# Retention followed by a two-layer leaky-ReLU network: who casts units 6 and 7, when units 10 and 11 are loaded, and where three tile bursts stand

## The chip, the cores and the metric

The kernel runs on one core of a Trainium2 chip. The metric is the device time of one execution in microseconds (us); lower is better. Five engines of the core run their own instruction lists side by side and meet at semaphores: TensorE (PE in the profile; PEld is its weight load), VectorE (DVE), ScalarE (ACT), GpSimd (POOL) and SyncE (SP, used here for transfers alone). Transfers are issued from the SP and POOL queues.

## The reference

```python
# q, k, v: 8 batches, 8 heads, 576 positions, 64 wide; float32
scores = scale * np.matmul(q, k.transpose(0, 1, 3, 2))
gamma = 1.0 - 2.0 ** (-5.0 - np.arange(H, dtype=np.float32))
Dmat = np.where(rel >= 0, gamma[:, None, None] ** rel[None, :, :], 0.0)
ret = scores * Dmat[None, :, :, :]
attn = np.matmul(ret, v)                      # retention, causal with decay
x = attn.transpose(0, 2, 1, 3).reshape(4608, 512)
h = x @ w_in                                  # 512 -> 2048
g = np.maximum(0.01 * h, h)
out = g @ w_out                               # 2048 -> 512, float32
```

## The kernel before

**Units.** The 4,608 tokens are cut into 36 units of 128 tokens (two chunks of 64). Retention is done chunk by chunk with a running state. For each unit u the steps are: `loads(u, eng)` brings k, q and v (three transfers of 256 KB, in this order) into float32 tiles `t`, of which five sets exist; `casts(u)` turns them into float16 (`cast_k` on ScalarE, L157; q and v multiplied by a decay table `cs` through `scaled`, L160, on VectorE where u < NEARLY and on GpSimd otherwise). The transposed q and k (`qkT`) come for u below NPE = 7 from TensorE (`transposes(u)`, L197, copied out at L203), and for later units from a transposing DMA that `cast_q` issues on SP (L171). `scores(u)` (L216, L225) fills one PSUM tile `sc`, of which there is one; `masks(u)` (L234) and `states(u)` (L252 to L257) read it on VectorE, so the next `scores` waits for them; `state_copy(u)` (L268) makes a float16 state, on ScalarE below NACT = 8 and on GpSimd from there on; `outputs(u)` (L323, L334) does 32 small matmuls into `ot`, ScalarE copies one half into `own` (L342), VectorE adds both into `xT` (L346).

**Groups.** The two layers run over groups of 256 tokens (two units). `g1_blocks(g)` gives eight blocks of 8 matmuls from `xT` and `w_in` into `hps` (L455, two buffers), each followed by ScalarE's leaky ReLU into `gt` (L462). `g2_blocks(g)` gives eight blocks of 4 matmuls from `gt` and `w_out` into `yps` (L478), a VectorE copy into `osb` (L488) and a store on SP (L490). The first group that goes wholly through the regular loop is group 3 (units 6 and 7), "layer one's fourth group"; its `g1_blocks(3)` needs `xT` of units 6 and 7.

**Order.** Every engine does its instructions in the order in which they are written; nothing reorders them. Up to L656 the order is written out by hand. From L657 `run(upto, *lists)` mixes the blocks of two lists by position and places "bursts" of unit work between them: burst n, from `steady(n)`, is `scores(n)`, `outputs(n-1)` (from n = 9 on), `masks(n)`, `states(n)`, then `casts(n+3)` (from n = 9 on), then `loads(n+6)` on SP. The call at L657 has ten blocks, eight of `g1_blocks(3)` and the last two of `g2_blocks(2)`, and bursts 8, 9 and 10; its blocks come in the order g1, g1, g2, g1, g1, g1, g1, g2, g1, g1. The line that places the bursts is

```python
run_steps(min(upto, a + -(-(upto - a) * (m + 1) // max(1, len(order) - 3)), done + 1))
```

With ten blocks and three bursts it puts burst 8 behind block 1, burst 9 behind block 3 and burst 10 behind block 5. In the next call burst 11 stands behind its first block, a `g1_blocks(4)` block that needs `xT` of units 8 and 9.

**GpSimd's queue.** Units 1 to 11 are loaded by GpSimd, with the weights between. Before a transfer `ring` keeps at most ten pieces of 256 KB in flight: it takes the oldest off by copying one element of it on GpSimd into `probe` (L132), which waits for that piece to land. Besides, the program as built has eight semaphores in turn for GpSimd's transfers, so each waits for the eighth before it. Behind L623 stand in GpSimd's list: loads of unit 9; casts of 6 and 7; loads of 10; casts of 8; loads of 11; casts of 9, 10 and 11. A load of unit u overwrites the float32 tiles of unit u-5, and so waits for that unit's casts.

Of the kernel before, what the change touches and what calls it, by code (L numbers as in the profile page):

```python
# [17 lines left out]
def kernel(  # L18
# [23 lines left out]
    nc = tc.nc  # L42
# [65 lines left out]

    NPE = 7
    NFIRST = 8  # L110
    NEARLY = 6
    NACT = 8
    NRING = 11
    t32 = {}
# [7 lines left out]
    def half(i):  # L122
        return slice(CH * i, CH * i + CH)
# [14 lines left out]
    def load(u, x, eng):  # L138
        t = ld_pool.tile([P, H, D], FP, name=f"t32_{x}")
        t32[u, x] = t  # L140
        (b0, c0), (b1, c1) = units[u]
        src = (q, k, v)[x]
        parts = [(t, b0, c0, P)] if b0 == b1 else [(t[0:CH], b0, c0, CH), (t[CH:P], b1, c1, CH)]
        for dst, b, c, n in parts:
            if eng is nc.gpsimd:
                ring(H * n * D * 4, dst[0:1, 0, 0:1])
            eng.dma_start(  # L147
                out=dst, in_=src[b, :, CH * c : CH * c + n, :].rearrange("h t d -> t h d")
            )

    def loads(u, eng):
        for x in (1, 0, 2):
            load(u, x, eng)

    def cast_k(u):
        qk16[u] = b_pool.tile([P, 2, H, D], F16, name="qk16")
        nc.scalar.copy(out=qk16[u][:, 1], in_=t32[u, 1])  # L157

    def scaled(u, x, out):
        (nc.vector if u < NEARLY else nc.gpsimd).tensor_tensor(  # L160
            out=out,
            in0=t32[u, x],
            in1=tab_sb[:, kind(u), x // 2, :].unsqueeze(2).to_broadcast([P, H, D]),
            op=MUL,
        )

    def cast_q(u):
        scaled(u, 0, qk16[u][:, 0])
        if u >= NPE:
            qkT[u] = b_pool.tile([P, 2, NP, P], F16, name="qkT")  # L170
            nc.sync.dma_start_transpose(  # L171
                out=qkT[u].rearrange("p x c t -> p (x c) t"),
                in_=qk16[u].rearrange("t x h d -> t (x h d)"),
            )

    def cast_v(u):
        v16[u] = b_pool.tile([P, H, D], F16, name="v16")
        scaled(u, 2, v16[u])

    def casts(u):  # L180
        if u >= NU:
            return
        cast_k(u)
        cast_q(u)
        cast_v(u)
# [86 lines left out]
    def st_before(u, j):  # L272

        if units[u][j][1] == 0:
            return zst
        if j:
            return st16[u][:, 0]
        return st16[u - 1][:, 1]
# [34 lines left out]
    def outputs(u):  # L313


        ot = ot_pool.tile([P, 2, 2 * NP, CH], FP, name="ot")
        own = ot[:, :, 0:NP]
        far = ot[:, :, NP : 2 * NP].rearrange("q r (s j) t -> q r s (j t)", j=2)
        for hp in range(NP):
            for h in (hp, hp + NP):  # L320
                o, c = divmod(h, NP)
                for j in range(2):
                    nc.tensor.matmul(  # L323
                        out=own[half(o), j, c, :],
                        lhsT=v16[u][half(j), h, :],
                        rhs=s16s[u][half(j), h % 2, h // 2, :],
                        start=True, stop=True, skip_group_check=True,
                    )
        for j in range(2):
            for s in range(2):  # L330
                for o in range(2):
                    for g in range(2):
                        p = 2 * o + s
                        nc.tensor.matmul(  # L334
                            out=far[half(o), g, s, half(j)],
                            lhsT=st_before(u, j)[half(g), p, :],
                            rhs=qkT[u][half(g), 0, p, half(j)],
                            start=True, stop=True, skip_group_check=True,
                        )
        t0 = P * u % XR  # L340
        tmp = a_pool.tile([P, NP, P], FP, name="own")
        nc.scalar.copy(  # L342
            out=tmp.rearrange("q c (j t) -> q c j t", t=CH),
            in_=own.rearrange("q j c t -> q c j t"),
        )
        nc.vector.tensor_tensor(  # L346
            out=xT[:, :, t0 : t0 + P].rearrange("q (s g) t -> q g s t", g=2),
            in0=far,
            in1=tmp.rearrange("q (s g) t -> q g s t", g=2),
            op=ADD,  # L350
        )
# [76 lines left out]
    ends = []  # L428
# [3 lines left out]
    done = 0  # L432

    def run_steps(upto):
        nonlocal done
        while done < upto:
            steps[done][1]()
            done += 1
# [4 lines left out]
    def g1_blocks(g):  # L443

        tok, t0 = sizes[g], starts[g]
        nf = TOK // tok

        def block(fb):
            if fb == 0:
                g_tiles[g] = g_pool.tile([P, NF, tok], F16, name=f"gt{tok}")  # L450
            hps = h_pool.tile([P, nf, tok], FP, name="hps")
            for f in range(nf):
                fc = fb * nf + f
                for c in range(NP):
                    nc.tensor.matmul(  # L455
                        out=hps[:, f, :],
                        lhsT=w_in16[:, c, fc * P : (fc + 1) * P],
                        rhs=xT[:, c, t0 % XR : t0 % XR + tok],
                        start=(c == 0),
                        stop=(c == NP - 1),  # L460
                    )
            nc.scalar.activation(  # L462
                out=g_tiles[g][:, fb * nf : (fb + 1) * nf, :], in_=hps,
                func=mybir.ActivationFunctionType.Lrelu,
            )

        return [lambda fb=fb: block(fb) for fb in range(NF // nf)]

    def g2_blocks(g, width=1):

        t0 = starts[g]

        def block(tbs, part):
            for f in range(4 * part, 4 * part + 4):
                for tb in tbs:
                    if f == 0:
                        y_cur[g, tb] = y_pool.tile([P, DM], FP, name="yps")
                    nc.tensor.matmul(  # L478
                        out=y_cur[g, tb],
                        lhsT=g_tiles[g][:, f, tb * P : (tb + 1) * P],  # L480
                        rhs=w_out16[:, f, :],
                        start=(f == 0),
                        stop=(f == NF - 1),
                    )
            if part == 3:
                for tb in tbs:
                    osb = o_pool.tile([P, DM], FP, name="osb")
                    nc.vector.tensor_copy(out=osb, in_=y_cur[g, tb])  # L488
                    r0 = t0 + tb * P
                    nc.sync.dma_start(out=out[r0 : r0 + P, :], in_=osb)  # L490

        return [
            lambda tb=tb, part=part: block(range(tb, tb + width), part)
            for tb in range(0, sizes[g] // P, width)
            for part in range(4)
        ]

    def run(upto, *lists):

        order = sorted(  # L500
            ((n + 0.5) / len(ls), x, n) for x, ls in enumerate(lists) for n in range(len(ls))
        )
        a = done
        for m, (_, x, n) in enumerate(order):
            lists[x][n]()
            run_steps(min(upto, a + -(-(upto - a) * (m + 1) // max(1, len(order) - 3)), done + 1))
        run_steps(upto)

    def g2_wide(tbs):
# [88 lines left out]
    def some(a, b):  # L598
        for m in range(a, b):
            wide[m]()  # L600

    g2 = g2_blocks(2)

    def more(blocks, a, b):
        for m in range(a, b):
            blocks[m]()
# [13 lines left out]
    scores(5)  # L620
    masks(5)
    states(5)
    loads(9, nc.gpsimd)  # L623
    casts(6)
    casts(7)
    some(9, 12)
    loads(10, nc.gpsimd)
    some(12, 13)
    outputs(5)
    some(13, 16)  # L630
    more(g1[2], 0, 1)
    transposes(6, sc_pool)
    casts(8)
    loads(11, nc.gpsimd)
    more(g1[2], 1, 3)
    scores(6)
    masks(6)
# [16 lines left out]
    more(g2, 1, 4)  # L654
    outputs(7)
    more(g2, 4, 6)  # L656
    run(ends[4], g1_blocks(3), g2[6:])  # L657
    for g in range(4, NG):
        run(ends[g + 1], g1_blocks(g), g2_blocks(g - 1))
    g2 = g2_blocks(NG - 1)  # L660
    run(ends[NG], g2[:4])
    for a, b in ((0, 3 * P), (3 * P, DM)):
        y = y_pool.tile([P, DM], FP, name="yps")
# [41 lines left out]
```

## Time and profile before

| what | value |
|---|---|
| median of 6 runs | 308.98 us (306.04, 306.64, 308.54, 309.42, 310.9, 311.46) |
| profiled execution, its own time | 306.04 us |
| its span, first to last instruction | 304.1 us |
| granted TensorE clock | 1.00 |
| busy PE / DVE / ACT / POOL | 291.6 / 107.0 / 138.1 / 121.5 us |
| bytes moved, mean rate | 50.26 MB, 165 GB/s |

How to read it: a busy time is the sum over an engine's instructions, a wait is idle time of an engine put down to the event that ended it. The chain of waits follows the work that ended last backwards from the last instruction. A mean over the span says little here, since the first quarter (loading, unit by unit) and the rest have different limits; so stages are read by windows of time.

### The profile page before, as it was taken

How to read it: one execution, taken by the hardware profiler on the slowest of the kernel's cores; microseconds unless marked ns; L12 is line 12 of the kernel's file. 1: busy time of each engine (PE TensorE's matmuls, PEld its weight loads, DVE VectorE, ACT ScalarE, POOL GpSimd, SP SyncE). 2: the span in 40 equal slices, each digit the busy share in tenths (PEclk: the TensorE clock that was granted, in tenths of full speed). 3: DMA queues.
4: the chain of work that ended last, by engine and by line, in shares of the span. 5: the costliest groups of instructions: out<-in, count | busy, mean ns of one | idle time of the engine just before them, and what ended most of it. 6: DMA issues, size and time to landing. Idle time of an engine off the chain costs nothing.

```text
span 304.1 us, 9489 instructions
## 1 busy us (share of the span) xinstructions
PE 291.6 (96%) x4169; PEld 197.1 (65%) x4169; DVE 107.0 (35%) x200; ACT 138.1 (45%) x240; POOL 121.5 (40%) x178
## 2 busy tenths in 40 slices
PE   3999999978999999999999999999999999999996
PEld 2478745736766666666666666666666666666663
DVE  1761153344442425152525143423333234331001
ACT  3577625834644444454535353535353534343320
POOL 8868869982533333333333333333333330000000
DMA  8999998899999995968496947685887221000011
GB/s 221 287 195 192 199 257 263 218 243 206 222 223 237 211 254 115 199 174 202 128 177 158 239 128 175 165 180 162 164 176 180 73 69 39 34 37 34 37 68 70
DMA packets 121400, 50.26 MB, mean 165 GB/s; under 512 B 110288, under 2 KB 114768, under 8 KB 121360
## 3 DMA queue, kind: packets, MB, share of 16 engines
q1 hardware_dynamic: 113952, 36.65, 52.1%
q0 software_dynamic: 6976, 12.85, 17.7%
q8 instruction: 32, 0.52, 0.7%
q10 hardware_dynamic: 432, 0.17, 0.3%
q14 instruction: 8, 0.07, 0.1%
HBM read 36.81 MB, written 9.44 MB: 152 GB/s over the span
## 4 chain that ended last, share of the span: by engine, by line
PE 76%; DMA 10%; POOL 9%; issue 2%; DVE 1%; ACT 1%; POOLq 0%; ACTq 0%
PE yps L478 34%; PE hps L455 34%; POOL t L147 6%; DMA w_out<-in_moe_w_out_dram 4%; DMA t<-in_k_dram 2%; PE sc L216 2%; DMA w_in<-in_moe_w_in_dram 2%; DMA t<-in_v_dram 2%; PE ot L334 1%; PE ot L323 1%; PE sc L225 1%; PE yps L665 1%; POOL qk L160 1%; POOL v L160 1%; POOL probe L132 1%
## 5 line engine op out<-in xcount | busy, mean ns | idle before, releaser
L455 PE MATMUL hps<-xT,w_in 128*128 128x256 f16 x1152 | 146.2, 273 | 2.5 <-DVE xT L346 1.9
L462 ACT ACTIVATE gt<-hps 128x512 f16<-128x512 f32 x144 | 85.7, 597 | 125.4 <-PE hps L455 125.1
L455 PEld LDWEIGHTS <-w_in 128*128 128x128 f16 x1152 | 112.1, 98 | 40.6 <-issue 3.0
L478 PE MATMUL yps<-w_out,gt 128*128 128x512 f16 x496 | 126.3, 380 | 0.0
L268 POOL CAST st<-s 128x512 f16<-128x512 f32 (+1 forms) x28 | 15.6, 557 | 137.4 <-DVE s L255 54.8
L478 PEld LDWEIGHTS <-gt 128*128 128x128 f16 x496 | 46.3, 98 | 34.3
L346 DVE TENSOR_TENSOR xT<-ot,own 128x512 f16<-128x512 f32 x32 | 22.1, 691 | 81.3 <-ACT own L342 81.3
L488 DVE COPY osb<-yps 128x512 f32<-128x512 f32 x31 | 21.3, 686 | 75.4 <-PE yps L478 75.4
L160 POOL TENSOR_TENSOR qk<-t,cs 128x512 f16<-128x512 f32 x30 | 31.3, 1043 | 1.2 <-DMA t<-in_q_dram 1.1
L160 POOL TENSOR_TENSOR v<-t,cs 128x512 f16<-128x512 f32 x30 | 31.3, 1042 | 0.0
L234 DVE TENSOR_TENSOR s<-sc,cs 128x512 f16<-128x512 f32 x36 | 24.6, 682 | 6.5 <-PE sc L225 5.0
L157 ACT CAST qk<-t 128x512 f16<-128x512 f32 x36 | 22.3, 621 | 4.2 <-DMA t<-in_k_dram 3.9
L342 ACT COPY own<-ot 128x512 f32<-128x512 f32 x32 | 18.7, 585 | 8.0 <-PE ot L334 6.1
L255 DVE TENSOR_TENSOR s<-sc,s 128x256 f32<-128x256 f32 x40 | 16.8, 419 | 0.7
L216 PEld LDWEIGHTS <-qkT 64*64 64x64 f16 x576 | 7.7, 108 | 11.3 <-issue 8.2
L216 PE MATMUL sc<-qkT 64*64 64x64 f16 x576 | 11.6, 199 | 1.8 <-DVE s L255 1.2
L147 POOL DMA_DIRECT2D t<-in_k_dram x12 | 10.5, 879 | 1.7 <-POOLq L689 0.8
L225 PE MATMUL sc<-v,qk 64*64 64x64 f16 x576 | 10.9, 194 | 0.0
L147 POOL DMA_DIRECT2D t<-in_v_dram x12 | 10.2, 850 | 0.3 <-issue 0.3
L147 POOL DMA_DIRECT2D t<-in_q_dram x12 | 10.2, 852 | 0.0
L523 PEld LDWEIGHTS <-gt 128*128 128x128 f16 x64 | 5.9, 98 | 6.3
L323 PE MATMUL ot<-s,v 64*64 64x64 f16 x512 | 9.8, 194 | 0.0
(52 smaller groups left out, 144.9 us busy)
## 6 DMA issues: line engine op xcount, KB each, us to landing
out_dram<-osb SPq DMA_DIRECT2D x35, 256.0 KB, 3.9
t<-in_k_dram SPq DMA_DIRECT2D x22, 256.0 KB, 3.3
t<-in_q_dram SPq DMA_DIRECT2D x22, 256.0 KB, 4.1
t<-in_v_dram SPq DMA_DIRECT2D x22, 256.0 KB, 4.1
t<-in_k_dram POOLq DMA_DIRECT2D x10, 256.0 KB, 5.2
t<-in_q_dram POOLq DMA_DIRECT2D x10, 256.0 KB, 5.5
t<-in_v_dram POOLq DMA_DIRECT2D x10, 256.0 KB, 5.4
w_in<-in_moe_w_in_dram POOLq DMA_DIRECT2D x8, 256.0 KB, 6.1
```

Of the source, the lines that this page charges most:

```text
L147: eng.dma_start(out=dst, in_=src[b, :, CH * c : CH * c + n, :].rearrange("h t d -> t h d"))
L157: nc.scalar.copy(out=qk16[u][:, 1], in_=t32[u, 1])
L160: (nc.vector if u < NEARLY else nc.gpsimd).tensor_tensor(out=out, in0=t32[u, x], in1=tab_sb[:, kind(u), x // 2, :].unsqueeze(2).to_broadca ...
L216: nc.tensor.matmul(out=a[half(j), g, 0, p, :], lhsT=qkT[u][half(g), 1, p, half(j)], rhs=qkT[u][half(g), 0, p, half(j)], start=True, stop=T ...
L234: nc.vector.tensor_tensor(out=s16s[u], in0=sc_tiles[u][:, :, 0], in1=mask_sb.unsqueeze(1).unsqueeze(1).to_broadcast([P, 2, NP, CH]), op=MUL,)
L255: nc.vector.tensor_tensor(out=dst, in0=st[:, j], in1=prev, op=ADD)
L342: nc.scalar.copy(out=tmp.rearrange("q c (j t) -> q c j t", t=CH), in_=own.rearrange("q j c t -> q c j t"),)
L346: nc.vector.tensor_tensor(out=xT[:, :, t0 : t0 + P].rearrange("q (s g) t -> q g s t", g=2), in0=far, in1=tmp.rearrange("q (s g) t -> q g s ...
L455: nc.tensor.matmul(out=hps[:, f, :], lhsT=w_in16[:, c, fc * P : (fc + 1) * P], rhs=xT[:, c, t0 % XR : t0 % XR + tok], start=(c == 0), stop ...
L462: nc.scalar.activation(out=g_tiles[g][:, fb * nf : (fb + 1) * nf, :], in_=hps, func=mybir.ActivationFunctionType.Lrelu,)
L478: nc.tensor.matmul(out=y_cur[g, tb], lhsT=g_tiles[g][:, f, tb * P : (tb + 1) * P], rhs=w_out16[:, f, :], start=(f == 0), stop=(f == NF - 1),)
L488: nc.vector.tensor_copy(out=osb, in_=y_cur[g, tb])
```

## The change

VectorE casts q and v of units 6 and 7, which GpSimd did; units 10 and 11 are issued by GpSimd straight behind unit 9, with no cast between them; the casts of unit 7 (ScalarE's k cast too) move behind `outputs(5)` in program order; and the one call at L657 places its bursts with `late=0`, which puts 8, 9 and 10 behind blocks 1, 4 and 7. No instruction's size changes, and the four casts keep their form.

```diff
-    NEARLY = 6
+    NEARLY = 8
...
-    def run(upto, *lists):
+    def run(upto, *lists, late=3):
...
-            run_steps(min(upto, a + -(-(upto - a) * (m + 1) // max(1, len(order) - 3)), done + 1))
+            run_steps(min(upto, a + -(-(upto - a) * (m + 1) // max(1, len(order) - late)), done + 1))
...
     states(5)
-    loads(9, nc.gpsimd)
+    for u in (9, 10):
+        loads(u, nc.gpsimd)
     casts(6)
-    casts(7)
     some(9, 12)
-    loads(10, nc.gpsimd)
+    loads(11, nc.gpsimd)
     some(12, 13)
     outputs(5)
+    casts(7)
     some(13, 16)
     more(g1[2], 0, 1)
     transposes(6, sc_pool)
     casts(8)
-    loads(11, nc.gpsimd)
...
-    run(ends[4], g1_blocks(3), g2[6:])
+    run(ends[4], g1_blocks(3), g2[6:], late=0)
```

GpSimd's list behind L623 then reads: loads of 9, 10 and 11; casts of 8, 9, 10 and 11. On SP the transposing DMA of unit 7 stood ahead of all four `osb` stores of groups 0 and 1; it now stands behind the first of them. `some(a, b)` are blocks of the second layer of groups 0 and 1 (L523, copied out at L532).

## Prediction

> **What bounds the kernel now.** I read the page's rate of work per stage first, by windows of time (columns: window, its length; busy us and count of PE, PEld, DVE, ACT, POOL; granted clock, DMA share, GB/s):
>
> ```profile
> 52.00:78.00 26.00, 22.42 (x433) 16.16 (x431) 10.53 (x20) 14.43 (x27) 19.18 (x27) 1.00 0.92 212
> 78.00:180.00 102.00, 102.00 (x1509) 69.46 (x1510) 37.32 (x71) 46.82 (x82) 35.92 (x42) 1.00 0.85 191
> ```
>
> From 78 us on TensorE never stands still: 102.00 of 102.00 us, at full clock. No edit here takes work from it, so whatever is won must be idle time before 78. TensorE's waits between 30 and 80 us (us in total, times, longest) are three:
>
> ```profile
> PE hps L455 <- DVE xT L346: 1.9, 1, 1.9
> PE sc L216 <- DVE s L255: 1.2, 1, 1.2
> PE hps L455 <- ACT gt L462: 0.5, 1, 0.5
> ```
>
> They sum to 3.57 us (1.87 + 1.16 + 0.54 in the timeline), the most this trace offers: 1.2% of 306.04. The chain of waits (start us, us, what) says what the largest is:
>
> ```profile
> 59.19 7.15 DMA t<-in_k_dram
> 66.34 0.02 issue
> 66.36 0.02 ACTq L157
> 66.38 0.04 issue
> 66.42 0.62 ACT qk L157
> 67.03 0.49 ACT own L342
> 67.53 0.02 issue
> 67.55 0.70 DVE xT L346
> 68.25 0.04 issue
> 68.29 1.03 PE hps L455 x8
> ```
>
> Unit 11's k is issued at 59.19 and lands at 66.34. ScalarE, in order, sits on its cast for 3.01 us; behind it is queued unit 7's `own` copy, ready since `outputs(7)` ended at 64.6; behind that VectorE's `xT` and the first block of layer one's fourth group. TensorE waits for a k tile that it needs some 15 us later. Why the load is that late is in GpSimd's timeline (start us, us, what):
>
> ```profile
> 50.02 1.05 POOL L160 TENSOR_TENSOR qk<-t,cs 128x512 f16<-128x512 f32 x1
> 51.03 1.04 POOL L160 TENSOR_TENSOR v<-t,cs 128x512 f16<-128x512 f32 x1
> 52.03 1.03 POOL L160 TENSOR_TENSOR qk<-t,cs 128x512 f16<-128x512 f32 x1
> 53.03 1.03 POOL L160 TENSOR_TENSOR v<-t,cs 128x512 f16<-128x512 f32 x1
> ```
>
> Four casts (units 6, 7) stand ahead of unit 10's loads, and two more (unit 8, 57.08 to 59.07) ahead of unit 11's.
>
> **Earlier loads.** Unit 9's last load ends at 49.93. A probe and an issue take 0.12 + 0.88, about 1.0 us (48.93 to 49.93). Six go through from there: unit 10's from 50.0, unit 11's k at about 53.1, the end at 56.0. Unit 11's k is thus issued 6.1 us earlier (six casts at 1.0 each); with the 7.15 us it took, it lands at 60.3. ScalarE reaches its cast after `state_copy(7)` at 63.4 and ends at 64.0, before `outputs(7)` does. Then `own` 64.6 to 65.2, `xT` to 65.9; TensorE finishes its second-layer blocks at 66.42 and waits no more: 1.87 us gone, with 0.5 us to spare, and landing has 4 us of slack. What is late next is the `own`–`xT` chain itself. The transfers fall where the DMA engines have room: between 52 and 56 us their share is 0.44 at 108 GB/s, against 1.02 at 334 GB/s from 44 to 48.
>
> The overwritten tiles: unit 11 needs unit 6's casts done. ScalarE's was done by 47.6; VectorE's two now run behind `states(5)`, from 46.4 to 47.7 if v of unit 6 (issued 40.81, median landing 5.2 us) is there. No wait.
>
> SP's queue: the transposing DMA of unit 7 goes at about 50.9, not 53.09; `scores(7)` wants it at 58.7. Units 8 to 11 follow GpSimd's casts, now 56.0 to 64, where unit 11's ended at 69.3; unit 8's has its q about 1 us earlier. Loads 12 and 13 on SP, behind unit 11's transposition, move from 69.65 to about 65, which hides them further. Unit 10's k had also been late by about 0.25 us at ScalarE (two casts in 1.37, where two at 47.01 take 1.13), so about 0.23 of the 0.54 us wait at 59.73 goes.
>
> **Four casts on VectorE.** By its own rows (L160 on VectorE, 0.68 to 0.69 us, pitch 0.60) they cost 2.5 us of VectorE, hidden in gaps: it idles from 46.39 to 48.45 and needs 1.3 for unit 6; unit 7's run behind `xT` of unit 5, 50.1 to 51.4, and push the second `osb` copy from 50.13 to 51.4, whose buffer is not wanted before 64. If the cover failed (v of unit 6 landing 8.4 us after issue or later, 49.25), `xT` of unit 5 would come after 51.3 and TensorE would wait one for one; the longest landing of these loads is 7.4 us, so I take 0, upper end 0.5. ScalarE's unit 7 cast behind `own` of unit 5 fits between 49.4 and 50.66: 0.
>
> VectorE casts beside GpSimd's list can lengthen both. The probes show it: 0.17 us as a rule, but one of 0.55 in the stretch 11.02 to 12.12 and one of 0.59 at 18.00, both while VectorE was at an L160 cast (17.88 to 18.56). The issues beside such casts keep 0.88 to 0.91 (29.34 to 31.99). So up to 0.42 us on each of four probes, 0 to 1.7 us on GpSimd; I take 0.8, which comes out of the 4 us of slack: 0 on TensorE.
>
> The Trainium skill, SBUF — State Buffer, section Who interferes with whom, has a rule against this edit: a VectorE instruction with two SBUF inputs and a GpSimd instruction that reads SBUF shut each other out, the second waiting for the first's end. The probe rows agree with it, and descriptor generation is spared there as in the rows of the issues; by its harsher sentence on a VectorE perf mode, which starves GpSimd's transfers, the four casts would hold GpSimd by 2.7 us, still inside the slack. The rule would speak loudest for casts beside casts, which no trace here shows.
>
> **The spread bursts.** Before, burst 10 follows burst 9 by 3.72 us, of which two blocks and the burst fill 2.56: `scores(10)` waits 1.16 for the one `sc` tile. The path burst start → `own` → `xT` → mask → states → next burst is 3.72 us (71.53 to 75.25) however the blocks stand. After, burst 8 to 9 has three blocks (3.1 us) where 2.27 are needed. From 9 to 10 there are three: 0.64 + 2.79 = 3.43, wait 0.29, so 0.87 is won. From 10 to 11, where there were six blocks, four: 0.84 + 3.58 = 4.42, needed 4.31 (75.25 to `states(10)` done at 79.42, and 0.14): no wait for `sc`, but GpSimd's `st` copy, 0.61, then holds `outputs(10)` as it holds `outputs(9)` now (0.84 for a burst against 0.64): 0.2 lost. The next group's first block needs `xT` of unit 9 2.3 us after burst 10 starts and comes after 3.4: covered.
>
> **Sum.** 1.87 + 0.23 + 0.87 − 0.2 = 2.77 us, about 2.8. The profiled execution would go from 306.04 to 303.2 (span 304.1 to 301.3). Both ends: 3.57 if every wait goes and no new one comes; 1.6 if the burst edit gives nothing and 0.5 is lost on `xT` of unit 5 (1.87 + 0.23 − 0.5).
>
> Against the median: that execution is the fastest of six, 2.94 below the median. Where the rest of them lose it no trace shows. The chain of waits is all GpSimd and DMA up to 68.29, TensorE is gapless at a clock of 1.00 from 78, so a slow transfer has one place to show: the wait for unit 11's k, for which the change makes 4 us of slack. If none of the 2.94 goes, the median becomes 306.2; if all, 303.2. I take half: 308.98 − 2.8 − 1.5 = 304.7.
>
> **Rivals.** *Another wait takes its place* (0.16). The removed wait was 1.87 us in which VectorE, GpSimd and SP caught up; with it gone the single `sc` tile sets bursts 9 to 11, or a transposed tile is late. For: burst 9 starts at 71.53, 0.15 after `states(8)` ended, so it is nearly tight already. Against: the spacing above. Then only some 0.9 of the 2.8 stay: 308.1.
>
> *GpSimd sticks in its loads* (slower, 0.12). Casts of units 8 to 11 are now behind six loads, each waiting for the eighth transfer before it. Unit 10's k needs unit 7's q, issued 42.56, by 50.0: 7.4 us, and the longest landing is 7.4. Crowded by these very loads, landings could stretch; at 11 us the last load ends near 59, unit 8's casts at 61, and its transposition (up to 7.9 us) at 68, 0.9 past `scores(8)` at 67.1. From there each us of landing costs about one: at 13 us the 2.8 are eaten, at 17 us the cost is 6.9 and the time 308.98 + 6.9 − 2.8 = 313.1. For: 334 GB/s and a share of 1.02 are already there from 44 to 48. Against: median 5.2 us there, and the empty stretch behind.
>
> *The bursts don't spread*: the built order has them behind blocks 1, 4, 7, so this falls away; if the spread is worth nothing, the gain is 2.1 and the time 305.4, inside the forecast.
>
> **How the numbers follow.** A run-to-run spread of this size cannot tell under about 1% from nothing: 305.9 to 312.1 is "the same". The forecast has 0.72; it spans 302.4 (3.57 with all of the surplus: 306.04 − 3.57) to 307.4 (308.98 − 1.6), and its middle, 304.7, is 1.2 below 305.9, so I give four fifths of it to faster: 0.58, and 0.14 to same. The first rival gives 0.16 same; the second is 0.12, taken as slower. The range, 302.0 to 309.0, holds the forecast and the first rival with some 0.4 to 0.9 of run-to-run spread beyond their ends, and leaves out the second.
>
> **What would show it.** Right: unit 11's k issued near 53 us; no wait of `hps` on `xT` near 66; the four casts on VectorE at 0.69 us; `scores(10)` waiting under 0.5 us; burst 11 near 78.5 instead of 81.42; the span near 301.3, gapless after. Wrong: GpSimd idle ahead of loads of 10 and 11 by more than 2 us; VectorE waiting on v of unit 6 past 49; a wait of `scores(8)` for its transposed tile; a span shorter by under 1 us; or the surplus of the slower runs staying whole, which puts the median near 306.2.

## The result, and the profile after

| | before | changed |
|---|---|---|
| median | 307.42 us (39 runs, 304.92 to 315.68) | 304.88 us (18 runs, 303.41 to 310.64) |
| ratio, with 95% interval | | 0.992 (0.9893 to 0.9946) |
| profiled execution, its own time | 306.04 us | 306.12 us |
| its span, mean granted clock | 304.1 us, 1.00 | 304.0 us, 0.994 |

The change makes the kernel 0.8% faster: 2.5 us of medians, and no more than the 1% named as the limit of telling. The ratios leave out executions over 1.5% above the fastest of their kernel, which the medians and ranges take in. The two profiled executions are equally long, so the second is not a typical one: TensorE's clock was halved in it for 3.4 us, which happens in some executions of both kernels.

The same stretches as before, by windows of time (window, its length; busy us and count of PE, PEld, DVE, ACT, POOL; granted clock, DMA share, GB/s), after:

```profile
52.00:78.00 26.00, 23.22 (x421) 15.79 (x419) 9.41 (x18) 13.49 (x25) 15.65 (x23) 0.93 1.07 244
78.00:180.00 102.00, 102.00 (x1520) 69.53 (x1521) 38.44 (x72) 47.27 (x82) 37.30 (x44) 1.00 0.86 188
```

From 78 us on nothing changed, 102.00 of 102.00. All that moved lies ahead of it, where the transfers' share rose from 0.92 to 1.07 and the clock fell to 0.93. Of TensorE's three waits one is left, and it has grown (us in total, times, longest us):

```profile
PE hps L455 <- ACT gt L462: 2.6, 1, 2.6
```

The chain of waits of the changed kernel (start us, us, what) says what is behind it:

```profile
52.11 7.45 DMA t<-in_k_dram
59.56 0.02 issue
59.58 0.02 ACTq L157
59.60 0.04 issue
59.64 0.62 ACT qk L157
60.25 0.51 ACT gt L462
60.76 0.04 issue
60.80 1.03 PE hps L455 x8
61.84 5.14 PE yps L478 x16
```

It has the shape of the chain before, one unit earlier: a k tile (now unit 10's), ScalarE's cast that waits for it, and behind that in ScalarE's list a leaky ReLU whose `hps` buffer TensorE needs. Then comes a line that has nothing to do with waiting, the 16 second-layer matmuls. By the timeline (start us, us, what), before and after:

```profile
60.60 3.62 PE L478 MATMUL yps<-w_out,gt 128*128 128x512 f16 x16
61.67 5.30 PE L478 MATMUL yps<-w_out,gt 128*128 128x512 f16 x16
```

The clock shows why, in windows of the changed kernel:

```profile
60.00:62.00 2.00, 1.20 (x10) 0.97 (x10) 0.25 (x1) 1.84 (x5) 2.00 (x3) 0.99 1.00 309
62.00:64.00 2.00, 2.00 (x7) 0.67 (x5) 1.79 (x4) 0.61 (x2) 2.00 (x3) 0.50 1.33 199
64.00:66.00 2.00, 2.00 (x8) 0.79 (x7) 0.00 (x0) 1.00 (x2) 2.00 (x3) 0.65 1.46 146
```

Seven matmuls in 2 us at a clock of 0.50: the wait of 2.61 us was followed by half speed, 1.7 us more.

### The profile page after: what moved, and what is told of

It reads as the page before. It is cut to its first block, busy times and chain, and to the rows that moved or that the text cites. A ratio compares the mean times of both kernels' runs of the same rounds, so it can differ in the third digit from the quotient of the medians.

```text
span 304.0 us, 9492 instructions
## 1 busy us (share of the span) xinstructions
PE 292.7 (96%) x4169; PEld 197.8 (65%) x4169; DVE 109.5 (36%) x204; ACT 138.3 (45%) x240; POOL 117.5 (39%) x174
## 4 chain that ended last, share of the span: by engine, by line
PE 78%; DMA 13%; POOL 5%; issue 2%; DVE 1%; ACT 1%; POOLq 0%; ACTq 0%
PE yps L478 37%; PE hps L455 34%; DMA w_out<-in_moe_w_out_dram 6%; POOL t L147 4%; DMA t<-in_k_dram 2%; PE sc L216 2%; DMA t<-in_v_dram 2%; DMA w_in<-in_moe_w_in_dram 2%; PE ot L334 1%; PE ot L323 1%; PE yps L665 1%; PE sc L225 1%; POOL probe L132 1%; DVE xT L346 0%; POOL st L268 0%
## 5 line engine op out<-in xcount | busy, mean ns | idle before, releaser
L478 PE MATMUL yps<-w_out,gt 128*128 128x512 f16 x496 | 128.0, 384 | 0.0
L478 PEld LDWEIGHTS <-gt 128*128 128x128 f16 x496 | 46.7, 99 | 35.5 <-issue 2.3
L160 POOL TENSOR_TENSOR qk<-t,cs 128x512 f16<-128x512 f32 x28 | 29.2, 1041 | 0.1
L160 POOL TENSOR_TENSOR v<-t,cs 128x512 f16<-128x512 f32 x28 | 29.1, 1041 | 0.0
L160 DVE TENSOR_TENSOR qk<-t,cs 128x512 f16<-128x512 f32 x8 | 5.5, 686 | 16.7 <-DMA t<-in_q_dram 16.7
L523 PEld LDWEIGHTS <-gt 128*128 128x128 f16 x64 | 5.9, 98 | 6.3
```

The lines of the kernel that those rows point to most:

```text
L160: (nc.vector if u < NEARLY else nc.gpsimd).tensor_tensor(out=out, in0=t32[u, x], in1=tab_sb[:, kind(u), x // 2, :].unsqueeze(2).to_broadca ...
L478: nc.tensor.matmul(out=y_cur[g, tb], lhsT=g_tiles[g][:, f, tb * P : (tb + 1) * P], rhs=w_out16[:, f, :], start=(f == 0), stop=(f == NF - 1),)
```

## The experiments

The runs are compared by ratio to the kernel before on the same chip, and by one stretch of the profile: from the start of `scores(7)` to the start of `scores(11)`, between which every edit acts. It took 22.69 us before (58.73 to 81.42) and 23.47 in the changed kernel's first profile.

Theory A: ScalarE, which does its list in order, holds TensorE up behind casts of tiles that are late; the change removes unit 11's and thins the bursts, and unit 10's stays. Rival B: the burst edit makes the whole gain. Rival C: the six early loads crowd the transfers, which makes something else late. Rival D: whatever is late next takes the place of the wait removed.

**The changed kernel once more, and its two halves.**

> The changed kernel once more. Theory A (two late loads: the change removes the wait for unit 11's k, and leaves a wait for unit 10's k in front of a leaky ReLU, whose size differs from run to run): 0.8% under before, no wait of hps on xT near 66 us, some wait of hps on gt near 60 us, between 0.3 and 2.9 us. Rival B (the burst edit alone makes the gain): the same time, but the wait near 60 us is always as long as what the load edit saved.

```diff
 # e2: before, with the burst edit alone
-    run(ends[4], g1_blocks(3), g2[6:])
+    run(ends[4], g1_blocks(3), g2[6:], late=0)
```

> Only late=0; casts and loads as before. Theory A: the wait of hps on xT near 66 us (about 1.9 us) stays, the wait of scores(10) falls from 1.16 to about 0.3 us, GpSimd's state copy holds burst 11 by 0.2: 0.5 to 0.9 us less, ratio 0.997 to 0.999. Rival B: the whole gain, ratio 0.992.

```diff
 # e3: the changed kernel, bursts as before
-    run(ends[4], g1_blocks(3), g2[6:], late=0)
+    run(ends[4], g1_blocks(3), g2[6:])
```

> Casts and loads as in the changed kernel, bursts as before. Theory A: 1.9 us less from the wait near 66 us, less what the wait for unit 10's k takes back: ratio 0.993 to 0.996; scores(10) waits about 1.2 us again. Rival B: ratio 0.999 to 1.001.

Measured: e1 0.9926 (0.9885 to 0.9967), e2 0.9977 (0.9935 to 1.0019), e3 0.9971 (0.9931 to 1.0011). Neither half alone is clear of 1; their product, 0.9948, is within e1's interval and just above that of the result (0.9893 to 0.9946). B falls: e2's interval begins above the 0.992 that B asked for, and by the profiles and the middle of the ratios the burst edit gives a quarter to a third. Where the time goes can be added up from the profiles, line by line. TensorE in e1 (start us, us, what; idle before, and what ended it):

```profile
58.84 0.34 PE L225 MATMUL sc<-v,qk 64*64 64x64 f16 x16
60.88 1.03 PE L455 MATMUL hps<-xT,w_in 128*128 128x256 f16 x8 [1.70 <-ACT gt L462]
61.75 0.38 PE L478 MATMUL yps<-w_out,gt 128*128 128x512 f16 x1
62.73 3.40 PE L478 MATMUL yps<-w_out,gt 128*128 128x512 f16 x15 [0.60 <-issue]
```

The wait behind unit 10's k is 1.70 us here, and a gap of 0.60 us has come behind the first of 16 equal matmuls, with no engine or buffer named. In us against before (minus is won), bursts being the stretch from `scores(8)` to `scores(11)`, 12.16 us before:

```
                            before    e1     e2     e3
wait on xT near 66 us        1.87     0      1.90   0
wait on gt near 60 us        0.54     1.70   1.07   0.31
gap in L478 near 62 us       0        0.60   0      1.29
scores(8) to scores(11)     12.16    11.22  11.33  12.17
sum of the changes                   -1.05  -0.27  -0.80
scores(7) to scores(11)     22.69    21.64  22.42  21.89
   against before                    -1.05  -0.27  -0.80
```

Four terms account for each stretch. The load edit removes 1.87 us and loses 1.06 (e3) to 1.76 (e1) of it again, the burst edit wins 0.83 to 0.94. One thing stays open: e1's ratio is worth 2.3 us (0.0074 of 307.37), its profile shows 1.05. Where the other executions win the rest, one profile of each can't show. The clock does not account for it: among the executions with a mean clock above 0.995 the median is 304.22 in e1 (9 of 12) and 306.55 before on that chip (20 of 35).

**Taking unit 10's k out of ScalarE's way.**

```diff
 # e4: the changed kernel
     casts(9)
-    casts(10)
 ...
+    casts(10)
     casts(11)
```

> The changed kernel with the casts of unit 10 put in front of those of unit 11, so that ScalarE meets unit 10's k some 6 us later in its list, behind the leaky ReLUs. Theory A: no wait of hps on gt near 60 us beyond 0.1 us, the clock stays at 1.00, the span is 301.3 or less (time 303.4 or less), ratio 0.985 to 0.990, and the executions near 310 us become rare. Rival C (unit 10's and 11's loads crowd the transfers, so that something else is late at once): the wait moves to another instruction between 60 and 70 us and the ratio stays at 0.992.

Measured: 0.9905 (0.9866 to 0.9943). In the profile the wait on `gt` is gone, the clock stays at 1.00, and the stretch is 20.13 us, 2.56 less than before (1.87 + 0.54 + 0.92 from the bursts, less a gap of 0.82, make 2.51). That is A's mechanism; its size is not seen in the time, for the median, 304.77, is e1's 304.75, and the intervals overlap. Two of its twelve executions have a mean clock below 0.995, against 11 of 32 of the changed kernel with e1: too few to tell. (The profile's span of 303.7 us holds 2.1 us lost ahead of the stretch.)

**Loading unit 11 later.**

```diff
 # e5: the changed kernel; e6: e4
-    loads(11, nc.gpsimd)
 ...
     casts(8)
+    loads(11, nc.gpsimd)
```

> The changed kernel, but unit 11's loads stand behind unit 8's casts in GpSimd's list (about 2 us later); unit 10's stay early. Theory C (six loads in a row crowd the transfers and delay others, among them the 16 KB block of instructions that TensorE needs at its second L478 matmul near 61 us): the block ends by 58.5 us, no 'issue' gap in L478; unit 10's k lands within 7 us; ratio 0.988 to 0.992. Rival (the crowding comes from the four stores and unit 10's loads, or the block's time is chance): the gap of 0.6 to 1.3 us and the wait on unit 10's k stay, ratio 0.992 to 0.993.

> Unit 10's casts in front of unit 11's (as in e4) and unit 11's loads behind unit 8's casts. Theory C: neither wait near 60 us nor gap near 62; stage from scores(7) to scores(11) 19.8 to 20.2 us against 22.7 before; ratio 0.986 to 0.990. Rival: as e4, stage 20.1 to 21 us with the gap, ratio 0.990 to 0.992.

Measured: e5 0.9999 (0.9962 to 1.0035), e6 0.9935 (0.9872 to 0.9998). e6's ratio stands on five of its twelve executions, and by the medians of all executions e5 has half of the gain (307.04 against 308.46 us, 0.995). C as I had put it, that unit 11's loads are the ones too many, is not borne out: the ratios don't fall, unit 10's k still takes 7.2 us to land in e5 and 9.1 in e6, and e6 keeps a gap of 1.04 us in L478. For C speaks only that in e5's profile the block of instructions ends at 58.22 and L478 has no gap. In e6's profile, of one of its longer executions (310.33 us), unit 11's k, issued at 57.4, lands at 68.4, and the wait of the kernel before is back. ScalarE, then TensorE, in e6:

```profile
68.51 0.62 ACT L157 CAST qk<-t 128x512 f16<-128x512 f32 x1 [5.79 <-DMA t<-in_k_dram]
```

```profile
70.39 1.87 PE L455 MATMUL hps<-xT,w_in 128*128 128x256 f16 x8 [3.49 <-DVE xT L346]
```

(In e5's profile the wait is at unit 10's k, 2.80 us; what its other executions lose is not seen.) The crowding itself is plain: transfers of 256 KB issued by GpSimd between 52 and 58 us land after 7.4 to 8.1 us in the changed kernel and 9.1 to 9.7 in e1, where those that the changed kernel issues between 48 and 50.1 take 4.5 to 5.1.

**The gap in L478.**

```diff
 # e7: e4
-    small_ones(60)
+    small_ones(64)
```

> e4 with 64 instead of 60 small warm-up matmuls at the start: four more weight loads and matmuls ahead in TensorE's list, 0.1 us of work. If the gap in L478 is TensorE waiting for its next block of instructions, the place moves four matmuls earlier: the last eight L455 matmuls ahead of L478 are split after the fifth, and TensorE resumes 1.46 us after the 16 KB block has landed, as in e1, e3 and e4. If the gap hangs on a buffer, a store or data of that second-layer block, it stays behind the first L478 matmul.

Inconclusive: in this profile (305.9 us) `scores(7)` waited 2.87 us for unit 7's transposed tile, which took 9.8 us to land; TensorE came too late to the place for any gap. What the other profiles hold is a coincidence, worked out from the trace's record of the queue "instruction":

```
             16 KB block landed   TensorE resumes   later by
e1               61.15                62.73           1.58
e3               60.60                62.06           1.46
e4               61.84                63.30           1.46
e6               59.87                61.29           1.42
e8               61.24                62.76           1.52
e10              61.18                62.40           1.22
e10, in L455     22.64                24.22           1.58
before           56.39          (no gap; at L478 60.60)
```

The block near 60 us takes some 1.0 us in each of these, as before; it starts later: 3.4 us ahead of `scores(7)` before, 0.3 us ahead to 2.0 us behind in these six profiles. So I read the gap as TensorE waiting for its next instructions, which come through the same crowded transfers. It is inferred from seven landings, not shown by an edit.

**A long idle stretch on purpose.**

```diff
 # e8: e4
     casts(11)
+    for _ in range(8):
+        nc.scalar.copy(out=spare, in_=idle)
```

> e4 with eight extra ScalarE copies of 0.5 us each in front of unit 7's own copy, so that TensorE idles about 3.7 us near 66 us, in the same place where it waited 1.87 us before. If a long idle stretch of TensorE alone halves its clock, every execution shows a mean clock of 0.995 or less and the profile a stretch at 0.50 shortly after the idle one, 3.4 us long; the time is 3.7 + 1.7 us over e4: 308 to 310. If the dips come from elsewhere, the clock is 1.00 in the profile and the time 307 to 308.5.

The copies add work and change no result. Measured: 1.0027 (0.9976 to 1.0079), 8 executions, 7 of them at a mean clock of 0.994 or less. The idle stretch I had aimed at came out at 0.33 us, as TensorE had already lost 2.77 us in the gap of L478, and the clock halved behind that one. So the edit did not set the length of the idle stretch; that rests on the profiles taken together, in the last section.

**Order alone, and order on top of the change.**

```diff
 # e9: before with late=0; e10: the changed kernel
     casts(9)
-    casts(10)
 ...
-    casts(11)
-    loads(12, nc.sync)
-    loads(13, nc.sync)
     more(g2, 1, 4)
     outputs(7)
+    casts(10)
+    casts(11)
+    loads(12, nc.sync)
+    loads(13, nc.sync)
     more(g2, 4, 6)
```

> The kernel before with late=0 and one more move: the casts of units 10 and 11 (and behind them loads 12 and 13) stand behind outputs(7), so that ScalarE makes unit 7's own copy before it meets unit 11's k. GpSimd keeps all its casts and issues its loads as before. Theory A (the gain is the removal of ScalarE's head-of-line waits, not of the loads' lateness itself): waits near 60 and 66 us gone though unit 11's k still lands at 66 to 67 us; no gap in L478, since the transfers are not crowded; stage scores(7) to scores(11) 20 us against 22.7; ratio 0.988 to 0.992, as good as the whole change. Rival D (unit 11's late transposed tile, or casts behind it, are late next): the wait moves to scores(10) or scores(11), ratio 0.995 to 1.000.

> The changed kernel with the casts of units 10 and 11 behind outputs(7) in the same way. Theory A: no wait on gt or xT near 60 to 68 us whatever unit 10's and 11's k do; the gap in L478 (0.6 to 1.3 us) may stay; ratio 0.985 to 0.990; fewer executions with a lowered clock than the 11 of 32 of the changed kernel. Rival D: no better than the changed kernel, 0.992.

Measured: e9 0.9992 (0.9956 to 1.0027), e10 0.9931 (0.9896 to 0.9967). Half of A holds in e9: the waits near 60 and 66 us are gone, there is no gap, and `scores(8)` starts 7.9 us behind `scores(7)` instead of 10.5. The rest is D. ScalarE in e9 (start us, us, what; idle before):

```profile
66.47 0.62 ACT L157 CAST qk<-t 128x512 f16<-128x512 f32 x1 [1.48 <-DMA t<-in_k_dram]
...
74.79 0.62 ACT L157 CAST qk<-t 128x512 f16<-128x512 f32 x1 [3.02 <-DMA t<-in_k_dram]
75.31 1.08 ACT L462 ACTIVATE gt<-hps 128x512 f16<-128x512 f32 x2
```

The wait has travelled along ScalarE's list to the next late tile, unit 12's k. Its load stands on SP behind unit 11's transposing DMA, and that stands behind GpSimd's casts of unit 11: issued at 70.79 here, 69.65 before, 68.15 in the changed kernel. TensorE idled 3.03 us and ran at half clock for 6.8 us, and eleven of the twelve executions have a mean clock of 0.994 or less. In this window order alone is worth nothing; the loads must come earlier too, which is what the change does. In e10's profile ScalarE casts units 10 and 11 without a wait, and it is again unit 12's k that TensorE loses 1.69 us behind, near 75 us. Its ratio is that of the changed kernel, as D has it; three of twelve executions have a lowered clock.

**The stores out of the way.**

```diff
 # e11: the changed kernel, e12: e10; eight osb buffers
 # g2_wide: instead of nc.sync.dma_start(out=out[r0 : r0 + P, :], in_=osb)
+                held.append((r0, osb))
 ...
 # e11 behind casts(10), e12 behind casts(9)
+    for r0, osb in held:
+        nc.sync.dma_start(out=out[r0 : r0 + P, :], in_=osb)
```

> The changed kernel with the four 256 KB stores of groups 0 and 1 issued on SP behind unit 10's transposing DMA (near 62 us instead of 49 to 54; eight osb buffers). If the stores are a good part of what crowds the loads from 50 to 60 us (1 of some 3 MB), unit 10's k lands within 6.5 us of its issue instead of 7.5 to 9, the block of instructions ends by 59 us, and the ratio is 0.985 to 0.990. If the loads and the transposing DMAs crowd each other alone, landings stay at 7.5 us or more and the ratio at 0.992.

> e10 with the four stores behind unit 9's transposing DMA. Theory A with crowding by the stores: none of the waits between 58 and 70 us, no gap in L478, stage 19.8 to 20.2 us, ratio 0.983 to 0.988: the best version. Otherwise as e10.

Measured: e11 0.9921 (0.988 to 0.9962), e12 0.9947 (0.9912 to 0.9983). In e11 the landings answer as the crowding by the stores would have it: unit 10's k takes 5.2 us (51.2 to 56.4), unit 11's 6.3 (54.2 to 60.5), the block of instructions ends at 57.84, and L478 has no gap. The time doesn't follow. ScalarE in e11:

```profile
57.06 1.14 ACT L157 CAST qk<-t 128x512 f16<-128x512 f32 x2
...
72.17 0.62 ACT L157 CAST qk<-t 128x512 f16<-128x512 f32 x1 [1.39 <-DMA t<-in_k_dram]
72.70 1.08 ACT L462 ACTIVATE gt<-hps 128x512 f16<-128x512 f32 x2
```

The casts of units 9 and 10 run without a wait, and 15 us on ScalarE waits for unit 12's k. Its load, behind the stores on SP, is issued at 67.93, no later than in the changed kernel (68.15); it is TensorE that is further on, with `scores(8)` at 66.25 instead of 69.99. So D holds here too, and the earlier loads of units 10 and 11 meet the next late tile. e12's profile has the shortest span of the study, 300.9 us, and one wait of 0.8 us left between 50 and 90, with a stretch of 19.60 us; but its ratio is no better than the changed kernel's. No version here beats the changed kernel beyond its interval; e4's 0.9905 is the lowest.

## Why the prediction came out as it did

**The time** (304.7 forecast, 304.88 measured) is right, and the way to it only in part: the gain was set 1.8 us too large (4.3 for 2.5) and the median to start from stood 1.6 too high (308.98 for 307.42), and the two cancel. That the time is so close is luck.

**Unit 11's k**, 1.87 us: right. No profile with the early loads of both units shows a wait on `xT` near 66 us (but for the 0.33 us that e8's copies make), and in e6, which gives up part of unit 11's earliness, it comes back. The step behind it failed in size: the issue was forecast at 53.1 and the landing at 60.3, with 4 us of slack. Measured were 55.11 and 62.9 in the changed kernel, 54.8 and 64.3 in e1. About 2 us of that is GpSimd arriving later from its weight transfers (unit 9's last load ends at 51.99, not 49.93); the rest is landing times of 7.8 and 9.5 us instead of 7.15. ScalarE came to the cast at 64.38 and 64.46, so of the slack 1.5 and 0.2 us were left.

**Unit 10's k** is the step that failed. I had it land in time and win 0.23 of the 0.54 us. So it went in e3, where it landed at 55.31 and 0.31 us of the wait were left. In the changed kernel its issue came earlier, 52.11 instead of 54.14, but it took 7.45 us instead of 4.4 and landed 1 us later than before (in e1 51.78 and 7.86). Part of the wait moved to it: 2.61 us there and 1.70 in e1. The windows have the reason; before and after, first line before:

```profile
52.00:56.00 4.00, 4.00 (x71) 3.45 (x69) 1.40 (x3) 2.85 (x7) 4.00 (x7) 1.00 0.44 108
```

```profile
52.00:56.00 4.00, 4.00 (x67) 3.40 (x65) 2.33 (x5) 2.86 (x6) 4.00 (x9) 1.00 1.13 276
56.00:60.00 4.00, 2.20 (x79) 1.84 (x77) 0.07 (x1) 1.80 (x4) 3.91 (x6) 1.00 1.04 368
```

I read the 0.44 as room and then gave the loads in it the landing times of a stretch that had room. They filled it (0.44 to 1.13). As an estimate, 168 GB/s more over 4 us is 0.67 MB, about 2 us at the 340 GB/s reached from 48 to 52 us, and by that much rather than by the six casts' 6.1 us the loads could land earlier. Measured, unit 11's k was issued 4.1, 4.4 and 6.4 us earlier than before in the changed kernel, e1 and e3, and landed 3.4, 2.1 and 4.7 us earlier (59.19 and 66.34 before; 55.11 and 62.92, 54.78 and 64.25, 52.80 and 61.63). The crowding stood among the rivals, with its price on unit 8's transposition; it bit at unit 10's k, unit 7's transposed tile (e7) and the instructions.

**The bursts**: right. Forecast 0.87 − 0.2 = 0.67; measured 0.83 (e2) and 0.94 (e1) from `scores(8)` to `scores(11)`. The wait of `scores(10)` fell from 1.16 us to under 0.1 in the changed kernel; bursts 9 and 10 are 3.60 us apart there, not the 3.72 that I took as fixed. GpSimd's state copy does hold `outputs(10)`: burst 11 fills 0.77 us instead of 0.64, where 0.84 had been forecast.

**The casts on VectorE**: right, 0.68 to 0.69 us, hidden, although v of unit 6 came late (cast at 48.04). Of the probes beside them one was lengthened. VectorE, then GpSimd, in the changed kernel:

```profile
50.45 0.68 DVE L160 TENSOR_TENSOR v<-t,cs 128x512 f16<-128x512 f32 x1
```

```profile
49.91 0.88 POOL L147 DMA_DIRECT2D t<-in_q_dram  x1
50.79 0.38 POOL L132 COPY probe<-t 1x1 f32<-1x1 f32 x1
```

The probe starts inside the cast and ends with it, 0.21 us late, and the issue ahead of it, beside this cast and the one before (49.85 to 51.13), keeps 0.88: this agrees with what the Trainium skill, SBUF — State Buffer, section Who interferes with whom, says of two SBUF inputs on VectorE against a GpSimd read. I had put 0.8 us on it.

**The median.** I took half of a 2.94 us surplus of six runs over the profiled one. With 39 runs the surplus is 1.38 (307.42 − 306.04), so the term of 1.5 was about that whole surplus. And the reason for it, that late transfers have one place to show, was wrong: they also show as half clock, which no row of the profile before had in it. Of 97 executions of the kernel before beside e1 to e12, 42 have a mean clock of 0.995 or less, with a median of 309.9 us; the other 55 have 306.8. In the changed kernel 8 of 20 have such a clock, with a median of 310.2, and the other 12 have 304.3: the gain is in the executions at full clock, and the others show none. The gain against the new median is 2.5 us, near the 2.8 of the sum. It lies just inside the bound of 1%, where 0.30 had been given, not beyond it, where 0.58 stood. (The middle of the forecast's 302.4 to 307.4 is 304.9, not the 304.7 that the shares were worked out from.)

## What to carry to other kernels

An empty stretch of the transfers can be filled, but landing times from a stretch with room don't hold once it is full: here issues that moved by 4.1 to 6.4 us moved the landing by 2.1 to 4.7. On an engine that works in order, a cast of a tile that is needed much later does not belong ahead of a copy that TensorE waits for; moved away, the wait turns up at the next such cast, so the list has to be followed to its end (unit 11, 10, then 12 here). A wait has to be priced with the clock behind it once it is longer than the 1.9 us that left the clock whole here.

## What the runs showed of the hardware

**TensorE's clock was halved after idle stretches of 2.6 us and more, not after those of 1.9 and less.** The longest idle stretch past 20 us and the clock behind it, one profile each:

```
1.00 throughout the stage:  before 1.87  e1 1.70  e2 1.90  e3 1.29  e4 0.82  e10 1.69  e11 1.44  e12 0.84
0.50 for 3.4 us:            changed 2.61  e5 2.80  e8 2.77
0.50 for about 6.8 us:      e6 3.49  e7 2.87  e9 3.03
```

The first 20 us are left out, because up to 10 to 13 us matmuls take twice as long in these profiles (four of 128x128 in 0.61 us, later eight in 0.62) while the column shows 1.00. By the mean clock of the windows, half clock begins 2.0 to 3.9 us after the idle stretch began: still within it in e5, e6, e7 and e9, 1.2 us behind its end in the changed kernel and 1.1 in e8. So most or all of it falls on the work behind the wait, where each 3.4 us cost 1.7. Three of the four early starts lasted twice as long; what decides that isn't shown. The Trainium skill, TensorE: Matmul & The Clock Gate, section What's actually happening, states half rate after an idle window of about 3.4 us of a free-running counter; the 0.50, the 3.4 us and a start that shifts against the idle stretch agree; the idle time that suffices is shorter here, 2.61 us.

**Instructions come through the transfers too.** The profile before has a queue "instruction" with 32 blocks of 16 KB. A block that landed 3.5 to 5.5 us later than before (56.39; 59.87 to 61.84 in the six profiles above) went with gaps of 0.34 to 2.77 us in the middle of a run of equal matmuls, put down to "issue"; with the stores moved it landed at 57.84 (e11) and 57.68 (e12), and there was no gap. By the inference above, a crowded stretch of loads can stop TensorE even where no data is late.
